# Layer one of the last two FFN blocks: seven products of half-size blocks instead of eight

## The chip, the cores and the metric

The kernel runs on one core of a Trainium2 chip. The metric is the device time of one execution in microseconds (us). PE is TensorE (matmuls), PEld its weight loads, DVE is VectorE, ACT is ScalarE, POOL is GpSimd, SP is SyncE, which issues nearly all DMAs. SBUF is the working memory, PSUM the eight accumulator banks (128 partitions x 512 fp32 each) that the matmuls write.

## The reference

```python
# attention with random features: q, k, v are (8 batches, 8 heads, 576, 64), omega is (128, 64)
q_p, k_p = phi(q_s), phi(k_s)                  # phi(x) = exp(x omega' - |x|^2/2 - max) / sqrt(128)
kv, z = einsum('bhsm,bhsd->bhmd', k_p, v), sum(k_p, axis=2)
x = num / den                                  # num = q_p kv, den = q_p z + 1e-6; x is 4608 tokens x 512
# feed-forward network (FFN)
h = x @ w_in                                   # 512 -> 2048
g = maximum(h, 0) + log1p(exp(-abs(h)))        # softplus
out = g @ w_out                                # 2048 -> 512
```

## The kernel before

**Tiling.** The 4608 tokens are cut into ten FFN blocks: two of 256 tokens, which run as a pair, and eight of 512 (`TB`). Called block 1 to block 8 here, these eight run one after the other. `w_in` and `w_out` are cut into 16 pieces of 128 hidden features (`NFC`). One step (`plan_step`) is one piece for one block: layer one makes `h` transposed, 128 hidden features x 512 tokens in one PSUM bank; ACT takes abs, exp and log, DVE adds max(h, 0) ("plus"); layer two multiplies by the piece's part of `w_out` and adds into four banks `acc`, one for each 128 tokens.

**Precision by splitting.** Each fp32 operand is held as a high and a low part (`xh`, `xl` for x; `gh`, `gl` for g; the two halves of the `wi` and `wo` tiles), and a product is three matmuls: high x high, high x low, low x high. Layer one of a step has four 128-deep chunks of x (`cc`), so 12 matmuls of 128x512 (L1040 to L1042). Layer two has four "tiles" of three matmuls each (L1069 to L1071), also 12. For each block that is 16 x 24 = 384 matmuls.

**x** lives in a ring of 1024 tokens (`RING`), that is two blocks: the attention of a later block writes x into the half of the ring that the block before last has left. x of a block comes from PE (`num` in `plan_x`, L992), which leaves it in two PSUM banks for each group of four heads; ACT rounds it to `xh` (L999) and DVE subtracts for `xl` (L1003). Attention of later batches runs between the FFN steps on all engines.

**Order.** Nothing is scheduled while the kernel runs, and each engine follows a written order. A planner (`in_order`) makes it before: every piece of work has a cost, the work that it waits for, the buffers and banks that it takes and gives back, and a due time; of what can start, the earliest due goes next. The numbers in `due + ...` and the tables `KEYS`, `QUERIES`, `IN`, `OUT` and `LATE` are its priorities. `with_fill` puts matmuls on constant data into early gaps of PE. POOL and DVE work marked `port=True` shares a port that the planner gives to one of them at a time.

**Banks.** Four of the eight banks are `acc`, two are `h` (layer one) and two are `at` (attention).

Of the kernel before, what the change touches and what calls it, by code (L numbers as in the profile page):

```python
# [10 lines left out]
F32 = mybir.dt.float32  # L11
# [8 lines left out]
P = 128  # L20
S = 576
# [11 lines left out]
AHEAD = 852.62  # L33
MARGIN = 0.00

LATE = {"num": 0.15, "turn": 52.71, "project": 0.86, "blocks": 0.82, "out": 0.35, "in": 1.69, "store": 1.22, "outer": 0.53}
# [11 lines left out]
PATIENCE = {"PE": 0.02, "DVE": 0.01, "ACT": 0.00, "POOL": 0.55, "SP": 1.42}  # L48
LEAN = {"DVE": 0.80, "POOL": 0.35, "ACT": 0.55}
KEYS = ((-43.36, -30.07, -31.94, -48.62, -93.75), (-78.36, -186.18, -77.84, -107.64, -136.45))  # L50
QUERIES = ((-77.13, -113.72, -93.37, -40.50, -2.02), (-251.59, -65.62, -225.91, -38.56, 57.66))
IN = (-72.00, -74.89, -153.56, 16.62, 44.96, -6.09, 5.92, 22.06, 77.07, 3.72, 131.98, 137.80, 388.30, 66.76, 84.33, 249.63)
OUT = (-29.34, 9.14, -28.60, 6.71, -28.19, -2.04, 43.69, 197.71, 17.60, 6.41, 70.70, 45.97, 65.95, 101.92, 218.09, 150.82)
SPREAD = ((0, 24.60), (-20.59, 57.76))
# [152 lines left out]
def favor_softplus_kernel(ctx, tc, q0, k0, qx, qy, kx, ky, vv, om, wi, wo, out):  # L207
# [104 lines left out]
    def plan_weights(nm, fc, due):  # L312
# [36 lines left out]
        def low_part(e):  # L349
# [5 lines left out]
            "SP", dma(0.65, 1.60, 1.7), due + 85.51, load, spare={} if last else {"w": 2},  # L355
# [5 lines left out]
        a = do(("ACT", "DVE"), (aw + 0.03, dw2), due + 4.63, low_bits, after=[l], port=True)  # L361
        b = do("ACT", aw + 0.03, due + 21.06, rebias, after=[l])
        c = do("DVE", dw, due + 12.79, joined, after=[a, b], port=True)
        d = do(
            ("ACT", "DVE"), (aw, dw2), due + 17.13, high_part, after=[c] + (in_w if last else []), take=[("w", box, "w")], port=True,
# [3 lines left out]
        return do(("DVE", "POOL"), (dw, pw), due + 19.28, low_part, after=[d], give=[(box, "raw")], port=True)  # L369
# [13 lines left out]
    def plan_unit(q, kind, us, due, early):  # L383
# [99 lines left out]
        def exponent(j):  # L483
# [13 lines left out]
            "SP", {"cost": 0.01, "wire": (0.0, 0.0, 2.00)} if apart else read(size), -99.0 if apart else due + 25.09, load, behind=prev.get("load"),  # L497
# [3 lines left out]
        if apart:  # L501
            ldv = [do("SP", read(P * 4 * VW), due - 47.33, lambda: nc.sync.dma_start(b["vt"], src[:, u, 1]), after=[ld])]
        if kind == "k" and not early:
            for i in range(len(us)):
                ldv.append(do(
                    "SP", dma(0.7, 1.0, 0.7), due + 76.79, lambda i=i: load_v(i), behind=ld, take=[("v", b, ("vs", i))]
                ))
        s = do(("POOL", "ACT"), (pool(w), act(w)), due + 87.38, squares, after=[ld])
        r, sm = None, [("sm", b, "sms")]
        if not cols:  # L510
            r = do("DVE", dve(w), due + 123.59, norms, after=[s], behind=prev.get("norms"), take=sm)
            prev["norms"] = r
# [31 lines left out]
        for i in range(len(us)):  # L544
            plan_queries(q, us[i], due + 27.53 * i, b, es, f"{nm}_{i}", i, i == len(us) - 1)

    def plan_split(q, kind, u, due):
# [59 lines left out]
        def exponent(t):  # L607
# [4 lines left out]
            "SP", read(n * (P + D) * P * 4), due - 147.41, load, behind=prev.get("load"), take=[("x", b, "x")],  # L612
        )
        prev["load"], ldv = ld, []
        if kind == "k":
            ldv = [do("SP", dma(0.7, 1.0, 0.7), due + 173.06, load_v, behind=ld, take=[("v", b, ("vs", 0))])]
        s = do(("POOL", "ACT"), (pool(n * D), act(n * D)), due + 105.53, squares, after=[ld])
        h = do(("ACT", "DVE"), (act(n * P), dve(n * P, 2)), due - 85.04, rounded, after=[ld], take=[("ts", b, "ts")], port=True)
        h = do(("DVE", "POOL"), (dve(n * P) + 0.12, 1.12 * pool(n * P)), due - 19.42, rest, after=[h, parted], give=[], port=True)
        r = do(  # L620
            "DVE", dve(n * D), due + 320.52, norms, after=[s, h], behind=prev.get("norms"), take=[("sm", b, "sms")],
# [4 lines left out]
            "PE", 0.118 * n, due - 37.94, project, after=[h], behind=(prev.get("project"), q.zc if kind == "q" else None),  # L626
# [5 lines left out]
        for t in range(n // 2):  # L632
            a = do(
                "ACT", act(2 * M, PSUM), due + 47.12, lambda t=t: aside(t), after=[p], behind=a,
                take=[] if t else [("ph", b, ("phs", 0))], spare={"ph": 1}, soon={} if t or n < 4 else {p: 0.22},
            )
            es.append(do("DVE", dve(2 * M), due - 26.11, lambda t=t: join(t), after=[a], give=[(b, ("ppb", t))]))
        m = do("DVE", dve(n * M), due - 38.93, maxima, after=es + [r])
        m = do("DVE", 0.33, due - 190.31, bias, after=[m], port=True)
# [20 lines left out]
    def plan_sums(q, keys, due, deps):  # L660
# [53 lines left out]
        if first:  # L714
            q.part = do("ACT", 0.29, due - 54.33, part, after=[m] + ([quads[q.n - 1].kvl] if q.n > 2 else []), give=[(y, "bank")])
            return
        a = do("DVE", 0.1, due - 223.16, z, after=[m, q.part], take=[("z", q.slots, "z")])
        q.kvl = do("DVE", 0.35, due - 64.91, whole, after=[m, a] + old, give=[(y, "bank")])
        a = do("DVE", 0.11, due + 312.18, z_turn, after=[a])
        r = do("SP", dma(2.0, 0.4, 1.4, 4), due + 87.99, out_z, after=[a], give=[(q.slots, "z")])  # L720
        q.zc = do("SP", dma(1.7, 1.6, 0.95), due - 9.18, in_z, after=[r], take=[("zb", q.slots, "zb")])

    def plan_early_keys(q, u, due, b, es):

        def outer():
# [12 lines left out]
            "PE", 0.87, due + 59.48, outer, after=es + [q.kvm], heat=2048,  # L738
# [14 lines left out]
        a = do("DVE", 0.07, due - 170.14, z, after=[q.kvm], take=[("zb", q.slots, "zb")])  # L753
        q.kvl = do("ACT", 0.32, due - 114.90, high, after=[q.kvm, a], give=[(q.slots, "kv")])
# [10 lines left out]
    def plan_queries(q, u, due, bu, es, nm, first, last):  # L765
# [46 lines left out]
        def in_blocks(qt, o, sizes):  # L812
# [13 lines left out]
            "DVE", 0.87, due + 26.67, den, after=es + [q.zc], steps=4, soon={es[1]: 0.62} if q.b > 1 and u < 4 else {},  # L826
# [475 lines left out]
```

## Time and profile before

| | us |
|---|---|
| median of 3 runs (lowest, highest) | 1007.83 (1006.66, 1009.06) |
| the profiled execution, its own time | 1009.49 |
| its span, first to last instruction | 1007.5 |
| PE busy in the span | 1000.7 (99%) |
| DVE busy, ACT busy, POOL busy | 736.3, 722.5, 173.7 |
| granted TensorE clock over the span | 1.000 of full speed (2.4 GHz) |

PE's busy time counts a matmul from its start to its modelled end. Matmuls overlap, so what a matmul costs in a row of them is read from the distance between two starts, not from its duration. Idle time of DVE or ACT costs nothing unless PE waits for it.

### The profile page before, as it was taken

Reading aid. Unit: us, or ns where it says so; the run is one execution under the profiler, and the core shown is the slowest. Engines: PE = TensorE matmul, PEld = TensorE weight load, DVE = VectorE, ACT = ScalarE, POOL = GpSimd, SP = SyncE. Lnnn points to the kernel's source line nnn. Section 1 sums busy time; section 2 is a strip of 40 time slices with the busy share of each in tenths; the row PEclk is TensorE's granted clock in tenths of the full one; section 3 lists DMA queues with packets and bytes.
Section 4 is the critical chain, followed back from the end, with each engine's and each line's share of the span. In section 5 each row is a group of like instructions: output and inputs, shape, how many; then the busy total and the mean of one; then the engine's idle time right before and its main releaser. Section 6 shows DMA issues by size and latency. Waiting matters only on the chain.

```text
span 1007.5 us, 17373 instructions
## 1 busy us (share of the span) xinstructions
PE 1000.7 (99%) x5536; PEld 842.5 (84%) x5536; DVE 736.3 (73%) x2203; ACT 722.5 (72%) x1767; POOL 173.7 (17%) x209
## 2 busy tenths in 40 slices
PE   9999999999999999999999999999999999999998
PEld 8999888888878888888878888888888888888886
DVE  5899986889889988897878778777788873223222
ACT  6999877878778878787777767777677664444443
POOL 3321332222202222422311001110002110000000
PEclk9999999999999999999999999999999999999999
DMA  9883366454465564453444433435353351001001
GB/s 344 295 286 121 105 158 157 132 149 139 119 183 153 133 171 123 151 144 108 139 127 125 125 103 110 126 93 134 95 155 92 93 123 48 1 1 42 1 1 43
DMA packets 117628, 124.50 MB, mean 124 GB/s; under 512 B 16288, under 2 KB 93728, under 8 KB 117536
## 3 DMA queue, kind: packets, MB, share of 16 engines
q1 hardware_dynamic: 117392, 123.26, 42.1%
q8 instruction: 44, 0.72, 0.3%
q14 instruction: 48, 0.39, 0.1%
q10 hardware_dynamic: 144, 0.13, 0.0%
HBM read 97.37 MB, written 25.98 MB: 122 GB/s over the span
## 4 chain that ended last, share of the span: by engine, by line
PE 96%; DMA 2%; DVE 1%; SPq 0%; ACT 0%; issue 0%; ACTq 0%
PE banks L1040 13%; PE banks L1069 13%; PE banks L1041 13%; PE banks L1042 13%; PE banks L1070 13%; PE banks L1071 13%; PE banks L673 6%; PE banks L585 5%; PE banks L992 2%; PE banks L442 1%; PE banks L732 1%; PE banks L949 1%; PE banks L872 1%; DMA rawo<-wo 1%; DMA xq<-q 1%; DMA xk<-k 0%
## 5 line engine op out<-in xcount | busy, mean ns | idle before, releaser
L1040 PE MATMUL banks<-xh,wi 128*128 128x512 f32 (+1 forms) x640 | 238.4, 372 | 0.3 <-DVE xl L926 0.3
L1041 PE MATMUL banks<-xl,wi 128*128 128x512 f32 (+1 forms) x640 | 236.2, 369 | 0.2 <-DVE xl L1003 0.2
L1042 PE MATMUL banks<-xh,wi 128*128 128x512 f32 (+1 forms) x640 | 235.9, 369 | 0.0
L1069 PE MATMUL banks<-wo,gh 128*128 128x512 f32 x576 | 228.7, 397 | 0.0
L1070 PE MATMUL banks<-wo,gh 128*128 128x512 f32 x576 | 225.1, 391 | 0.0
L1071 PE MATMUL banks<-wo,gl 128*128 128x512 f32 x576 | 224.8, 390 | 0.0
L1059 ACT CAST gh<-u 128x512 fp32r<-128x512 f32 (+1 forms) x142 | 82.7, 583 | 110.8 <-PE banks L1070 109.3
L1055 DVE SCALAR_TENSOR_TENSOR u<-banks,u 128x512 f32<-128x512 f32 (+1 forms) x160 | 101.0, 632 | 78.7 <-ACT u L1052 77.4
L1063 DVE TENSOR_TENSOR gl<-u,gh 128x512 fp32r<-128x512 f32 (+1 forms) x128 | 85.2, 666 | 88.6 <-ACT gh L1059 86.2
L1040 PEld LDWEIGHTS banks<-xh,wi 128*128 128x128 f32 x640 | 120.5, 188 | 22.2 <-issue 1.5
L1042 PEld LDWEIGHTS banks<-xh,wi 128*128 128x128 f32 x640 | 120.5, 188 | 20.7
L1041 PEld LDWEIGHTS banks<-xl,wi 128*128 128x128 f32 x640 | 120.7, 189 | 18.8 <-DVE xl L1003 0.5
L1069 PEld LDWEIGHTS banks<-wo,gh 128*128 128x128 f32 x576 | 108.2, 188 | 23.7 <-issue 4.3
L1071 PEld LDWEIGHTS banks<-wo,gl 128*128 128x128 f32 x576 | 108.1, 188 | 23.5
L1046 ACT ACTIVATE u<-banks 128x512 f32<-128x512 f32 (+1 forms) x160 | 90.0, 562 | 52.3 <-DVE gl L1063 32.2
L1070 PEld LDWEIGHTS banks<-wo,gh 128*128 128x128 f32 x576 | 108.4, 188 | 19.1
L1049 ACT ACTIVATE u<-u 128x512 f32<-128x512 f32 (+1 forms) x160 | 95.2, 595 | 3.0
L1052 ACT ACTIVATE u<-u 128x512 f32<-128x512 f32 (+1 forms) x160 | 95.0, 594 | 2.8
L609 ACT ACTIVATE phq<-phq,smq 128x128 f32<-128x128 f32 x216 | 70.4, 392 | 19.1 <-DVE smq L605 18.9
L609 ACT ACTIVATE phk<-phk,smk 128x128 f32<-128x128 f32 x216 | 71.2, 393 | 16.7 <-DVE smk L605 16.3
L781 DVE CUSTOM_DVE_ANT_0 restq<-phq,zb 128x128 f32<-128x128 f32 x280 | 72.1, 291 | 6.4 <-ACT phq L609 4.9
L791 POOL TENSOR_TENSOR phq<-phq,dnq 128x512 f32<-128x512 f32 (+1 forms) x42 | 37.8, 900 | 195.2 <-DVE dnq L787 77.9
(147 smaller groups left out, 1455.8 us busy)
## 6 DMA issues: line engine op xcount, KB each, us to landing
xk<-ky SPq DMA_DIRECT2D x48, 384.0 KB
xq<-qy SPq DMA_DIRECT2D x48, 384.0 KB
qdq<-restq SPq DMA_DIRECT2D x56, 256.0 KB
out<-o SPq DMA_DIRECT2D x36, 256.0 KB
vk<-vv SPq DMA_DIRECT2D x70, 130.0 KB
rawi<-wi SPq DMA_DIRECT2D x16, 512.0 KB
rawo<-wo SPq DMA_DIRECT2D x16, 512.0 KB
q<-qdq SPq DMA_DIRECT2D x64, 128.0 KB
```

What stands on the lines that cost most here:

```text
L609: nc.scalar.activation(b["ph"][:, c], b["ph"][:, c], AF.Exp, bias=b["sm"][:, 2, c : c + 1])
L1040: nc.tensor.matmul(b["h"], wh, xh[:, cc, t], start=cc == 0, stop=False)
L1041: nc.tensor.matmul(b["h"], wh, xl[:, cc, t], start=False, stop=False)
L1042: nc.tensor.matmul(b["h"], wl, xh[:, cc, t], start=False, stop=cc == NCC - 1)
L1046: nc.scalar.activation(b["u"], b["h"], AF.Abs)
L1049: nc.scalar.activation(b["u"], b["u"], AF.Exp, scale=-1.0)
L1052: nc.scalar.activation(b["u"], b["u"], AF.Ln, bias=1.0)
L1055: nc.vector.scalar_tensor_tensor(b["u"], b["h"], 0.0, b["u"], ALU.max, ALU.add)
L1063: return (nc.vector if e == "DVE" else nc.gpsimd).tensor_tensor(b["gl"], b["u"], b["gh"].bitcast(F32), ALU.subtract)
L1069: nc.tensor.matmul(acc[tt], gh, w2[fc][:, 0], start=fc == 0, stop=False)
L1070: nc.tensor.matmul(acc[tt], gh, w2[fc][:, 1], start=False, stop=False)
L1071: nc.tensor.matmul(acc[tt], gl, w2[fc][:, 0], start=False, stop=fc == NFC - 1)
```

## The change

The last two blocks (7 and 8) no longer run one after the other. `plan_pair` takes both at once in eight rounds (j = 0 to 7); a round treats the pieces j and j + 8 together. Layer one is then a product of two 2 x 2 block matrices: of the weights, A11 and A12 (piece j, first and second 256 rows of x's features) and A21, A22 (piece j + 8); of x, B11, B21 (block 7, first and second 256 features) and B12, B22 (block 8). In place of eight half-depth products it uses seven (Strassen's scheme in Winograd's form), six matmuls each (L1196): p1 = A11 B11, p2 = A12 B21, p3 = S4 B22, p4 = A22 T4, p5 = S1 T1, p6 = S2 T2, p7 = S3 T3.

- The weights' sums S1 to S4 are made in each round by DVE or POOL from the re-joined pieces (L1309 to L1323), and split again into high and low (L1326 to L1338); they overwrite pieces of `wi` that are no longer read, and a tile `L`.
- x's sums T1 to T4 are made once (`plan_late_x`): DVE adds and subtracts in the two PSUM banks in which block 8's x stands (L1084); ACT rounds (L1120, L1145) and DVE subtracts (L1125, L1148) for high and low parts.
- p1, p6, p5 and p3 follow each other in one bank, A, and p7 and p4 in another, C; p2 has B. Between, the bank is copied to SBUF (`copied`: s1 after p1, s2 after p6, s7 after p7; L1202) and DVE adds (`added`, L1205: c11 = B + s1, c22 = A + s7, c21 = C + s2).
- The four results go through softplus as before (`plan_g`). Block 7's g ("near") is used by layer two in the same round; block 8's g ("far") is stored over used pieces of `wi` and multiplied after the rounds, one 128-token tile after the other.
- The banks `at` are free for layer one then (`room["hp"]`), and small SBUF tiles of the attention serve as buffers (`room["two"]`).
- The planner's other priorities are new numbers throughout; of these the diff below shows two lines.

```diff
-PATIENCE = {"PE": 0.02, "DVE": 0.01, "ACT": 0.00, "POOL": 0.55, "SP": 1.42}
+PATIENCE = {"PE": 0.03, "DVE": 0.01, "ACT": 0.00, "POOL": 1.54, "SP": 1.49}
...
-            if w > 256:
+            if q.b * S + o == B * S - TB:
+                plan_late_x(q, due, o, w, any_, qc)
+            elif w > 256:
                 plan_x(q, due, o, w, any_, qc, len(kinds))
...
+        steps = {
+            3: [lambda p: tt(y[p], late["x"][:, p], ALU.subtract, p)],
+            2: [lambda p: tt(y[p], x11[0][:, p], ALU.add, p), lambda p: tt(y[p], x11[1][:, p], ALU.add, p)],
+            4: [lambda p: tt(x21[0][:, p], y[p], ALU.subtract, p), lambda p: tt(y[p], x21[1][:, p], ALU.add, p)],
+            1: [lambda p: tt(late["x"][:, p], x11[0][:, p], ALU.subtract, p), lambda p: tt(y[p], x11[1][:, p], ALU.subtract, p)],
+        }
...
+        def product(k, j, b, key, fresh):
+            if fresh:
+                b[key] = bank(f"h_{i}_{j}_{key}", b["bank", key])
+            for kk in range(2):
+                ah, al = left(k, j, b, kk)
+                bh, bl = right[k](kk)
+                for n, (x, y) in enumerate(((ah, bh), (ah, bl), (al, bh))):
+                    nc.tensor.matmul(
+                        b[key], x, y, start=fresh and not kk and not n, stop=kk == 1 and n == 2, skip_group_check=True
+                    )
+
+        def copied(e, b, key, name, nm):
+            b[name] = two(f"{name}{nm}", b["tag", name])
+            (nc.scalar.copy if e == "ACT" else nc.vector.tensor_copy)(b[name], b[key])
+
+        def added(out_, a_, b_):
+            nc.vector.tensor_tensor(out_, a_, b_, ALU.add)
...
+            p6 = prod(6, "A", False, due + 12.49, [s1, l12] + late["done"][2])
+            s2 = do(*cp, due - 35.25, lambda e, b=b, nm=nm: copied(e, b, "A", "s2", nm), after=[p6], take=[("two", b, ("tag", "s2"))])
+            p7 = prod(7, "C", True, due + 61.20, [l34] + late["done"][3], kind=hp, give=tg)
+            s7 = do(*cp, due + 21.51, lambda e, b=b, nm=nm: copied(e, b, "C", "s7", nm), after=[p7], take=[("two", b, ("tag", "s7"))])
+            p5 = prod(5, "A", False, due + 9.80, [s2] + late["done"][1], give=[(b, ("tag", "L"))])
+            c22 = do("DVE", dve(TB), due + 59.59, lambda b=b: added(b["s7"], b["A"], b["s7"]), after=[p5, s7])
+            p4 = prod(4, "C", False, due - 43.85, [s7] + late["done"][4])
+            c21 = do("DVE", dve(TB), due + 4.91, lambda b=b: added(b["C"], b["C"], b["s2"]), after=[p4, s2], give=[(b, ("tag", "s2"))])
+            p3 = prod(3, "A", False, due + 23.71, [c22] + late["B22"])
...
+        if i >= len(sizes) - 2:
+            if i == len(sizes) - 1:
+                k0_ = k
+                plan_pair(i - 1, t0 - TB, lambda j: FIRST + 2.00 * (k0_ + j * 16 / 3), chain)
+            t0 += n
+            continue
...
+    room["hp"] = room["h"] + room["at"]
+    room["th"], room["two"] = room["ph"][:4], room["ph"][4:] + room["zb"] + room["ts"] + room["t2"]
```

The first place is PE in the last two blocks. Before, a step there is layer two of one piece, of which the end stands here, and layer one of another (`wi_170` is piece 2), of which the first three matmuls stand here:

```order
L1069 MATMUL banks<-wo_1431,gh_13_10289 128x512
L1070 MATMUL banks<-wo_1431,gh_13_10289 128x512
L1071 MATMUL banks<-wo_1431,gl_13_10291 128x512
L1040 MATMUL banks<-xh,wi_170 128x512
L1041 MATMUL banks<-xl,wi_170 128x512
L1042 MATMUL banks<-xh,wi_170 128x512
```

After, this is the shortest hand-off in rounds 1 and 2: the end of p7 of round 1 (`th` is T3, `wi_448` piece 1), all of p1 of round 2 (`wi_170`), and the start of p4 of round 1 (`wi_792`, piece 9):

```order
L1196 MATMUL banks<-th_9786,wi_448 128x512
L1196 MATMUL banks<-xh,wi_170 128x512
L1196 MATMUL banks<-xl,wi_170 128x512
L1196 MATMUL banks<-xh,wi_170 128x512 x2
L1196 MATMUL banks<-xl,wi_170 128x512
L1196 MATMUL banks<-xh,wi_170 128x512
L1196 MATMUL banks<-xh,wi_792 128x512
L1196 MATMUL banks<-xl,wi_792 128x512
```

p4 goes into the bank in which p7 stands, so the copy s7 must lie between them; six matmuls of p1 stand there. Before, no matmul of a step waits for a copy of its own bank.

The second place is DVE after PE's last `num`, which brings block 8's x. Before, that is two subtractions for `xl` among the steps' plus and `gl`:

```order
L1055 SCALAR_TENSOR_TENSOR u_2_9842<-banks,u_2_9842 128x512
L1103 COPY o_0_9858<-banks 128x256
L1003 TENSOR_TENSOR xl<-banks,xh 128x512 x2
L1103 COPY o_1_9875<-banks 128x256
L1103 COPY o_2_9877<-banks 128x256
L1059 CAST gh_1_9887<-u_1_9799 128x512
L1063 TENSOR_TENSOR gl_1_9889<-u_1_9799,gh_1_9887 128x512
```

After, x's sums stand there (`b` is B22, `th` T3, `xh` and `xl` the ring, `x` block 8's first half set aside):

```order
L1148 TENSOR_TENSOR b_9740<-banks,b_9739 128x512
L1424 SCALAR_TENSOR_TENSOR u_14_9711<-banks,u_14_9711 128x512
L1084 TENSOR_TENSOR banks<-banks,x_9562 128x512
L1148 TENSOR_TENSOR b_9740<-banks,b_9739 128x512
L1084 TENSOR_TENSOR banks<-banks,x_9562 128x512
L1125 TENSOR_TENSOR th_9772<-banks,th_9771 128x512
L1084 TENSOR_TENSOR banks<-banks,xh 128x512
L1125 TENSOR_TENSOR th_9787<-banks,th_9786 128x512
L1084 TENSOR_TENSOR banks<-banks,xl 128x512
L1084 TENSOR_TENSOR banks<-banks,xh 128x512
L1428 CAST gh_14_9809<-u_14_9711 128x512
L1084 TENSOR_TENSOR banks<-banks,xl 128x512
```

The two subtractions of before have become a run of sums in the banks, and p6 of round 0 waits for the one that ends in T2.

## Rows read from the trace of the kernel before

**Rows 1.** The page's first part: busy us, share of the span, instructions.
```profile
PE 1000.7 (99%) x5536; PEld 842.5 (84%) x5536; DVE 736.3 (73%) x2203; ACT 722.5 (72%) x1767; POOL 173.7 (17%) x209
```

**Rows 2.** Stages: length, busy us of PE, PEld, DVE, ACT, POOL; PE's clock.
```profile
0.00:837.40 837.40, 835.01 (x4808) 705.73 (x4808) 688.49 (x2129) 646.21 (x1639) 173.68 (x209) 1.00 0.50 145
837.40:1003.10 165.70, 165.70 (x730) 136.73 (x729) 47.42 (x74) 75.72 (x127) 0.00 (x0) 1.00 0.04 14
...
300.00:350.00 50.00, 50.00 (x251) 41.43 (x250) 47.24 (x151) 42.06 (x112) 11.81 (x12) 1.00 0.54 147
750.00:800.00 50.00, 50.00 (x252) 42.43 (x251) 38.73 (x120) 35.68 (x83) 7.33 (x10) 1.00 0.32 87
```

**Rows 3.** All waits of PE: engine, line, releaser; us, times, longest.
```profile
PE banks L1191 <- DVE small L260: 1.1, 1, 1.1
PE banks L442 <- ACT xk L492: 0.3, 1, 0.3
PE banks L1040 <- DVE xl L926: 0.3, 1, 0.3
PE banks L992 <- DVE phk L594: 0.3, 1, 0.3
PE banks L1041 <- DVE xl L1003: 0.2, 1, 0.2
```

**Rows 4.** Timeline of the last block: start us, us, instruction; nine matmuls apart.
```profile
986.63 0.39 PE L1040 MATMUL banks<-xh,wi 128*128 128x512 f32 x1
...
988.67 0.39 PE L1040 MATMUL banks<-xh,wi 128*128 128x512 f32 x1
```

**Rows 5.** Groups by line and form, 850 to 1008: busy us, mean ns.
```profile
L1042 PE MATMUL banks<-xh,wi 128*128 128x512 f32 x104 | 40.5, 389 | 0.0
...
L1063 DVE TENSOR_TENSOR gl<-u,gh 128x512 fp32r<-128x512 f32 x29 | 20.1, 692 | 56.6 <-ACT gh L1059 56.5
...
L1055 DVE SCALAR_TENSOR_TENSOR u<-banks,u 128x512 f32<-128x512 f32 x27 | 18.7, 691 | 50.9 <-ACT u L1052 50.9
L1059 ACT CAST gh<-u 128x512 fp32r<-128x512 f32 x28 | 17.5, 624 | 57.8 <-PE banks L1070 57.8
L1049 ACT ACTIVATE u<-u 128x512 f32<-128x512 f32 x27 | 17.1, 632 | 0.8
...
L1046 ACT ACTIVATE u<-banks 128x512 f32<-128x512 f32 x27 | 16.2, 598 | 20.5 <-DVE gl L1063 20.5
...
L1059 DVE CAST gh<-u 128x512 fp32r<-128x512 f32 x1 | 0.4, 428 | 1.4 <-PE banks L1070 1.4
```

**Rows 6.** Timeline of the last microseconds: the last matmul and two copies behind it.
```profile
1002.72 0.39 PE L1071 MATMUL banks<-wo,gl 128*128 128x512 f32 x1
...
1003.15 0.42 DVE L1103 COPY o<-banks 128x256 f32<-128x256 f32 x1 [0.26 <-PE banks L1071]
1003.66 0.37 ACT L1106 COPY o<-banks 128x256 f32<-128x256 f32 x1 [0.36 <-DVE o L1103]
```

**Rows 7.** The chain that ended last, 57 to 62: start us, us, what.
```profile
59.44 1.30 DVE xl L926 x2
60.74 0.04 issue
60.78 0.39 PE banks L1040
```

**Rows 8.** Instructions of L992, PE: ns min/median/max, first and last start us.
```profile
L992 PE MATMUL banks<-q,kvs x192: 272/379/483, 142.4 to 837.1; 128*64 128x256 f32 x96, 128*64 128x192 f32 x32, 128*64 128x128 f32 x32, 128*64 128x320 f32 x32
```

**Rows 9.** Groups by form: DVE from 100 to 800, POOL over the whole span.
```profile
L1063 DVE TENSOR_TENSOR gl<-u,gh 128x512 fp32r<-128x512 f32 x75 | 53.2, 709 | 26.2 <-ACT gh L1059 24.2 <-PE banks L585 0.9
...
L791 POOL TENSOR_TENSOR phq<-phq,dnq 128x512 f32<-128x512 f32 x28 | 29.1, 1042 | 123.6 <-DVE gl L1063 28.2 <-ACT xk L565 22.4 <-ACT u L1049 20.4
L1063 POOL TENSOR_TENSOR gl<-u,gh 128x512 fp32r<-128x512 f32 x17 | 22.1, 1297 | 24.3 <-DVE dnq L781 7.2 <-ACT gh L1059 5.6 <-PE banks L585 4.6
...
L567 POOL TENSOR_TENSOR xq<-xq 128x256 f32<-128x256 f32 x20 | 12.6, 628 | 93.6 <-DVE tk L579 34.2 <-DMA qdq<-restq 19.9 <-DVE phq L791 9.9
```

More of the change, by code (lines that the diff above doesn't have):

```diff
@@ L368, in plan_weights @@
             in_w.append(d)
-        return do(("DVE", "POOL"), (dw, pw), due + 19.28, low_part, after=[d], give=[(box, "raw")], port=True)
+        return do(("DVE", "POOL"), (dw, pw), due + 18.49, low_part, after=[d], give=[(box, "raw")], port=True)
     class Quad:
@@ L611, in plan_split @@
         ld = do(
-            "SP", read(n * (P + D) * P * 4), due - 147.41, load, behind=prev.get("load"), take=[("x", b, "x")],
+            "SP", read(n * (P + D) * P * 4), due - 152.50, load, behind=prev.get("load"), take=[("x", b, "x")],
         )
@@ L615, in plan_split @@
         if kind == "k":
[L616 to L619, printed above, removed]
+            ldv = [do("SP", dma(0.7, 1.0, 0.7), due + 211.07, load_v, behind=ld, take=[("v", b, ("vs", 0))])]
+        s = do(("POOL", "ACT"), (pool(n * D), act(n * D)), due + 66.28, squares, after=[ld])
+        h = do(("ACT", "DVE"), (act(n * P), dve(n * P, 2)), due - 154.74, rounded, after=[ld], take=[("ts", b, "ts")], port=True)
+        h = do(("DVE", "POOL"), (dve(n * P) + 0.12, 1.12 * pool(n * P)), due + 0.33, rest, after=[h, parted], give=[], port=True)
         r = do(
-            "DVE", dve(n * D), due + 320.52, norms, after=[s, h], behind=prev.get("norms"), take=[("sm", b, "sms")],
+            "DVE", dve(n * D), due + 323.70, norms, after=[s, h], behind=prev.get("norms"), take=[("sm", b, "sms")],
             give=[(b, "x")],
@@ L751, in high @@
             nc.scalar.activation(q.kvs[:, :, 0:D], q.kv[:, :, 0:D], AF.Copy, scale=rm)
[L753 to L754 removed]
+        a = do("DVE", 0.07, due - 157.56, z, after=[q.kvm], take=[("zb", q.slots, "zb")])
+        q.kvl = do("ACT", 0.32, due - 138.62, high, after=[q.kvm, a], give=[(q.slots, "kv")])
     def chunks(b):
@@ L928, in plan_early_x @@
         t = do(
-            "PE", 0.45 if tail else 0.46, due - 161.70, turn, after=[d for _, d in rows], heat=1024, behind=prev.get("turn_x"),
+            "PE", 0.45 if tail else 0.46, due - 194.03, turn, after=[d for _, d in rows], heat=1024, behind=prev.get("turn_x"),
             take=[("any", y, "b")], give=[(b, "x") for b, _ in rows],
@@ L932, in plan_early_x @@
         prev["turn_x"] = t
-        h = do(("DVE", "ACT"), (dve(2 * w), act(2 * w, PSUM)), due - 167.20, high, after=[t])
-        l = do("DVE", dve(2 * w), due - 105.45, low, after=[h], give=[(y, "b")])
+        h = do(("DVE", "ACT"), (dve(2 * w), act(2 * w, PSUM)), due - 170.43, high, after=[t])
+        l = do("DVE", dve(2 * w), due - 52.32, low, after=[h], give=[(y, "b")])
         for p in range(2):
@@ L1109, in store @@
                 nc.sync.dma_start(out[t0 + tt * P : t0 + (tt + 1) * P, :], o["t"])
-            a = do("DVE", 0.34, due - 26.74, left, after=[ends[tt]], take=[("ph" if last else "t2", o, "s")])
-            r = do("ACT", 0.27, due - 108.35, right, after=[ends[tt]] if last and tt == n // P - 1 else [a], give=[(box, ("acc", i, tt))])
-            do("SP", dma(0.25, 0.8, 1.05), due - 111.08, store, after=[a, r], give=[(o, "s")], late=LATE["store"])
+            a = do("DVE", 0.34, due - 71.60, left, after=[ends[tt]], take=[("ph" if last else "t2", o, "s")])
+            r = do("ACT", 0.27, due - 107.26, right, after=[ends[tt]] if last and tt == n // P - 1 else [a], give=[(box, ("acc", i, tt))])
+            do("SP", dma(0.25, 0.8, 1.05), due - 112.46, store, after=[a, r], give=[(o, "s")], late=LATE["store"])
     assert NQ == 2
@@ L1150, in favor_softplus_kernel @@
     PAIR = 2
-    GAP = 15.46
-    PACE = 5.66
+    GAP = 7.56
+    PACE = 5.05
     t0, k, j = 0, 0, 0
```

415 lines of the change are left out of this document (350 added, 65 removed).

## The prediction

> **What bounds the kernel now.** I read the page's first part, then the busy time by stage, PE's waits, the timeline of the last block, and the groups by line. PE is busy for 1000.7 of 1007.5 us [rows 1] and in every stage shown it is busy all the time at full clock, 1.00 of 2.4 GHz [rows 2]. All its waits come to 2.0 us, of which the last, 0.2 us, is for an `xl` [rows 3]. Busy time alone would not prove a bound, since matmuls overlap; the timeline does: from 986.63 to 988.67 us nine matmuls start in 2.04 us, 0.2267 us each, while one lasts 389 ns [rows 4, 5]. From the last `num` (837.4) to the end of PE 730 matmuls take 165.7 us, 0.2270 each [rows 2]: that stage is a stream of matmuls with nothing between them. So fewer matmuls there are less time, as long as the others can still follow each other without a gap. DVE is busy for 688.5 of 837.4 us (82%) before 837.4 and 47.4 of 165.7 (29%) after it; ACT 77% and 46%; POOL does nothing after it [rows 2].
>
> **What goes.** Before, blocks 7 and 8 have 16 steps each with 12 matmuls in layer one: 384. After, 8 rounds of 7 products with 6 matmuls: 336. The written order has 4840 matmuls before and 4792 after, 48 fewer, all of 128x512, and the same 12 on constant data. 48 x 0.2267 = 10.88 us. The Trainium skill (TensorE: Matmul & The Clock Gate, Back-to-back issue gap) gives 512 columns 512/2.4 + 2.5 = 215.8 ns from start to start. Its sum would be 10.4 us, and the row, 0.2267, decides against it.
>
> **What comes on the other engines, in the rounds.** PE's work in a round is 42 matmuls of layer one and 24 of block 7's layer two, 66 x 0.2267 = 15.0 us. By the order, ACT has in the eight rounds 24 copies and 32 abs from banks or copies (598 ns), 64 exp and log (632 ns) and 34 roundings (624 ns) [rows 5]: 33.5 + 40.4 + 21.2 = 95 us of 120, 79%. DVE has 95 operations of 128x512 (692 ns), 16 of 256 columns (0.42 us, the copy in [rows 6]) and 14 quick casts (428 ns) [rows 5]: 65.7 + 6.7 + 6.0 = 78 us, 65%. Neither is the bound of a round; they hide behind PE if no single hand-off is late.
>
> **The hand-offs.** A copy must lie between two products of one bank. After the last matmul's start, 1002.72, a copy starts at 1003.15 [rows 6], 0.43 later, that is 0.20 after its slot of 0.227; the copy takes 0.60 (ACT from a bank, [rows 5]); a result reaches PE 0.04 later (60.74 to 60.78, [rows 7]). That makes 0.84 us. Of the 24 copies, eight (s7 of rounds 0, 1, 3, 4, 6, 7 and s2 of rounds 2 and 5) have six matmuls between, 1.36 us, the others twelve or more. So 0.52 us are left at the tightest, and one ACT operation (0.63) that has just started in front makes PE late by up to 0.11: eight times that is 0.9. Two in front would be 0.74, or 5.9 in all. From p4 to layer two of the same result lie at the least 24 matmuls, 5.44 us (rounds 0, 3 and 6); the chain is 0.20 + c21 0.69 + 0.60 + 0.63 + 0.63 + plus 0.69 + rounding 0.62 + low part 0.69 = 4.75, and seven hand-offs of some 0.03 to 0.09 (1003.57 to 1003.66, [rows 6]), about 5.15. That leaves 0.3. I take 0.4 us of PE waiting for all of these.
>
> **The sums of x.** They stand between the last `num` and p6 of round 0. PE has 13 tiles of layer two, p1 and p2 there, 51 matmuls, 11.56 us. DVE has 15 operations up to the last low part of T2: 14 x 0.69 + 0.43 = 10.1 us, after 0.20 for the last matmul and 0.60 for ACT's first rounding: 10.9. Two such operations in a row take 1.30 us, not 1.38 [rows 7], so 0.61 each, and then it is 9.8. The slack is 0.7 to 1.8 us. Up to p5 of round 0 DVE has 22 us and PE 25.8. One form has no row: DVE writing into a bank (14 sums, six of them ahead of p6, and 16 of the L1205 sums). The nearest rows are a bank read at 691 ns and two SBUF operands at 692; the low end is the quick cast, 428 ns, the high end two passes, 1.38 us. At the low end p6 waits for nothing. At the high end p6 is late by 6 x 0.69 less the slack, 2.3 to 3.4 us, p5 by 14 x 0.69 - 3.8 = 5.9 in all, and with c21 0.69 longer three rounds lose 0.4 each: 7.1. I take 0.69, since both rows agree on it, and 0.5 us of waiting at p6 for the chance that it is a little more.
>
> **Attention ends earlier.** Block 8's x is now needed before round 0. After the last `num` PE has 60 + 336 + 384 = 780 matmuls, 176.8 us, where it had 165.7; with an end 10 us earlier its last matmul must start at some 816 (1002.95 - 10 - 176.8) instead of 837.1 [rows 8]. DVE's 688.5 us then need 84% of the time instead of 82% [rows 2]. At 94% of DVE (300 to 350) PE still had no gap [rows 2]; I take nothing, and the price if this cover is gone is a rival below.
>
> **The rest.** The other priorities change the order only slightly ahead of the first FFN step: the same DMAs, a few swapped, and the same number of matmuls ahead of it. With waits of 2.0 us in all [rows 3] there is at most that to gain, and I take 0 with 1.5 either way. The end keeps its chain (matmul, two half copies one after the other, store); the last store is now alone, where four followed each other; I take 0 and up to 0.4 less.
>
> **The sum**, against the profiled execution: 1009.49 - 10.88 + 0.4 + 0.5 = 999.5. The median of the runs is 1.66 below that execution, so 997.8 us.
>
> **Rivals.**
> *PE waits in the rounds or at p6* for what is added above: speaking for it, the tight places and the form without a row; against it, 79% and 65%. Price 3 to 8 us (5.9 by the copies, 7.1 by the sums): 1000 to 1005.
> *POOL takes DVE's port.* POOL has 41 operations in the rounds: 22 by 1.04 to 1.30 us, 16 by 0.63 and 3 low parts by 1.30, some 40 us of 120 [rows 9]. If a DVE operation with two SBUF operands must wait for POOL's to end, it meets one in a third of the cases and waits 0.65 on average; the 16 low parts of block 7's g have the least cover: 16 x 0.33 x 0.65 = 3.4 us, so 1000.4. The rows speak against it: the same DVE operation takes 709 ns where POOL works and 692 where it does nothing [rows 5, 9], 17 ns, that is 0.9 us for some 55 such operations on an engine with 35% free. The Trainium skill (SBUF — State Buffer, Who interferes with whom) says that the two engines share a port pair and that the later one waits out the other's whole instruction when a DVE instruction has two SBUF inputs. By that rule this rival holds wherever the written order does not keep the two apart; the trace so far shows only the 17 ns.
> *Slower: attention does not get done earlier.* If DVE, at 94% in places, can't be packed closer, p6, p7 and p4 of round 0 wait for block 8's x. All 21 us unabsorbed give 997.8 + 21 = 1019; the change loses from 11 us on, half of it, and with 15 it is 1013. Against it: DVE is free for 149 us before 837.4 [rows 2].
> *It doesn't do what it says*, because PE isn't bound by matmuls: against it 0.2270 us over 730 of them. The time would be 1008.
>
> **Chances.** The forecast 0.70, with a range of its own of 995.5 to 1000 (no waits and 1.5 less from the order: 995.5; 2 us more of waits: 1000). Waits in the rounds 0.17; POOL's port 0.05; slower 0.04; no change 0.04. The range, 995.0 to 1003.0, leaves out the upper part of the second case and the two last. A measurement of this kernel can tell 0.2%, 2 us, from no change: faster 0.92, same 0.04, slower 0.04.
>
> **What would show it.** Right: the last stage of PE with starts 0.227 apart and 780 matmuls after the last `num`, whose last matmul starts at 813 to 818; PE's waits under 3 us in all; L1084 and L1205 at 0.65 to 0.75 us. The second case would show PE waiting on L1196 for ACT s (L1202) or on DVE (L1125), the third DVE low parts well over 0.7 us, the fourth one long wait at round 0. The prediction is wrong if PE waits for 5 us or more in the last two blocks, or if its stream there is not 0.227 apart.

## The result, and the profile after

The changed kernel took 994.88 us (median of four runs, 994.32 to 997.79) where the kernel before, on the same chip, took 1008.44 (1006.66 to 1014.88): ratio 0.986, interval 0.9812 to 0.9908. That is 13.6 us less where 10 were forecast, and 0.12 us under the range. The profiled execution after took 997.79 us, 11.70 less than the one before (1009.49). The first thing to settle is why these two differences aren't the same.

The first part of the page after, to set beside [rows 1]:

```profile
PE 989.3 (99%) x5488; PEld 832.2 (84%) x5488; DVE 772.7 (78%) x2273; ACT 729.7 (73%) x1801; POOL 235.2 (24%) x261
```

48 matmuls fewer; DVE and POOL do 36 and 62 us more, and PE is still busy for 99% of the span. The stages after (length, busy us of PE, PEld, DVE, ACT, POOL; PE's clock), beside [rows 2], the first from behind the last `num` to the end of PE:

```profile
813.94:992.14 178.20, 178.20 (x782) 146.37 (x780) 93.62 (x157) 99.25 (x179) 47.53 (x44) 1.00 0.05 17
850.00:900.00 50.00, 50.00 (x220) 41.03 (x219) 29.61 (x49) 33.64 (x60) 21.36 (x22) 1.00 0.00 0
```

The rounds are a stream of matmuls too, 0.2273 us each in the second row. All waits of PE, beside [rows 3]:

```profile
PE banks L1568 <- DVE small L260: 1.1, 1, 1.1
PE banks L442 <- ACT xk L492: 0.8, 1, 0.8
PE banks L1409 <- DVE xl L928: 0.3, 1, 0.3
PE banks L994 <- DVE phk L594: 0.3, 1, 0.3
PE banks L1409 <- DVE u L1424: 0.2, 1, 0.2
```

L1196 is not among them: no product waits. They come to 2.7 us in all (forecast: under 3). The `num` of block 8 (L1045, instruction by line: ns min/median/max, first and last start), beside [rows 8]:

```profile
L1045 PE MATMUL banks<-q,kvs x32: 379/379/430, 790.6 to 813.6; 128*64 128x256 f32 x32
```

The last starts at 813.6, where 816 (813 to 818) was forecast. The new forms on DVE from 800 on (busy us, mean ns), beside [rows 5, 9]:

```profile
L1205 DVE TENSOR_TENSOR banks<-banks,s 128x512 f32<-128x512 f32 x16 | 11.1, 696 | 8.6 <-PE banks L1196 8.6
...
L1084 DVE TENSOR_TENSOR banks<-banks,xl 128x512 f32<-128x512 f32 x6 | 4.2, 692 | 0.1
...
L1084 DVE TENSOR_TENSOR banks<-x,xh 128x512 f32<-128x512 f32 x2 | 2.1, 1070 | 0.0
```

DVE writing into a bank takes 0.69 us, as taken; the 1070 has another cause (below). The end, beside [rows 6]:

```profile
991.75 0.39 PE L1255 MATMUL banks<-wo,wi 128*128 128x512 f32 x1
992.18 0.37 ACT L1271 COPY o<-banks 128x256 f32<-128x256 f32 x1 [10.09 <-PE banks L1255]
992.58 0.42 DVE L1268 COPY o<-banks 128x256 f32<-128x256 f32 x1 [10.90 <-ACT o L1271]
```

The last matmul starts 10.97 us earlier than before. From it to the end of the span are 4.25 us where there were 4.77.

**The start is the surprise.** The first matmul of layer one, at 60.78 before [rows 7], starts at 59.44 after, though the written order of PE is the same up to 13 us. Busy time by stretch from 5 to 20 us, of before:

```profile
5.00:10.00 5.00, 5.00 (x42) 4.25 (x40) 2.56 (x7) 3.22 (x9) 2.80 (x4) 1.00 1.08 359
10.00:15.00 5.00, 5.00 (x35) 4.15 (x37) 2.25 (x7) 2.92 (x11) 3.94 (x8) 1.00 1.10 370
15.00:20.00 5.00, 4.88 (x70) 4.75 (x66) 3.54 (x12) 3.59 (x13) 0.12 (x1) 1.00 1.03 392
```

and of after:

```profile
5.00:10.00 5.00, 5.00 (x42) 4.25 (x40) 2.56 (x7) 3.17 (x9) 2.69 (x4) 1.00 1.08 361
10.00:15.00 5.00, 5.00 (x49) 4.15 (x51) 2.64 (x9) 2.91 (x11) 2.89 (x6) 1.00 1.08 374
```

PE is busy all the time in both, but gets through 35 matmuls from 10 to 15 us in the one and 49 in the other. The clock column says 1.00 there, yet the trace has no record of a granted clock before 17.2 us in before and 13.4 us in after; until then the matmuls are twice as far apart: the first 128x512 ones, on constant data, start 0.43 us from each other, where [rows 4] have 0.2267. PE runs at 1.2 GHz first, and the moment it goes to 2.4 GHz was another in these two executions.

### The profile page after: what moved, and what is told of

Read it like the earlier page. It is cut to its first block, busy times and chain, and to the rows that moved or that the text cites. A ratio compares the mean times of both kernels' runs of the same rounds, so it can differ in the third digit from the quotient of the medians.

```text
span 996.0 us, 17456 instructions
## 1 busy us (share of the span) xinstructions
PE 989.3 (99%) x5488; PEld 832.2 (84%) x5488; DVE 772.7 (78%) x2273; ACT 729.7 (73%) x1801; POOL 235.2 (24%) x261
## 4 chain that ended last, share of the span: by engine, by line
PE 96%; DVE 1%; ACT 1%; DMA 1%; issue 0%; SPq 0%; ACTq 0%
PE banks L1409 10%; PE banks L1438 10%; PE banks L1410 10%; PE banks L1411 10%; PE banks L1439 10%; PE banks L1440 10%; PE banks L1196 8%; PE banks L673 5%; PE banks L585 5%; PE banks L1254 3%; PE banks L1253 3%; PE banks L1255 3%; PE banks L442 2%; PE banks L994 2%; PE banks L732 1%; PE banks L951 1%
## 5 line engine op out<-in xcount | busy, mean ns | idle before, releaser
L1409 PE MATMUL banks<-xh,wi 128*128 128x512 f32 (+1 forms) x512 | 189.0, 369 | 0.5 <-DVE xl L928 0.3
L1410 PE MATMUL banks<-xl,wi 128*128 128x512 f32 (+1 forms) x512 | 186.3, 364 | 0.1
L1411 PE MATMUL banks<-xh,wi 128*128 128x512 f32 (+1 forms) x512 | 186.1, 363 | 0.0
L1438 PE MATMUL banks<-wo,gh 128*128 128x512 f32 x448 | 178.2, 398 | 0.0
L1439 PE MATMUL banks<-wo,gh 128*128 128x512 f32 x448 | 175.3, 391 | 0.0
L1440 PE MATMUL banks<-wo,gl 128*128 128x512 f32 x448 | 175.0, 391 | 0.0
L1409 PEld LDWEIGHTS banks<-xh,wi 128*128 128x128 f32 x512 | 96.4, 188 | 18.4 <-issue 2.3
L1411 PEld LDWEIGHTS banks<-xh,wi 128*128 128x128 f32 x512 | 96.4, 188 | 15.6
L1410 PEld LDWEIGHTS banks<-xl,wi 128*128 128x128 f32 x512 | 96.6, 189 | 13.6 <-DVE xl L1005 0.4
L1438 PEld LDWEIGHTS banks<-wo,gh 128*128 128x128 f32 x448 | 84.2, 188 | 18.1 <-issue 3.4
L1439 PEld LDWEIGHTS banks<-wo,gh 128*128 128x128 f32 x448 | 84.4, 188 | 14.1
L1424 DVE SCALAR_TENSOR_TENSOR u<-banks,u 128x512 f32<-128x512 f32 (+1 forms) x128 | 78.8, 617 | 18.9 <-ACT u L1421 17.9
L1432 POOL TENSOR_TENSOR gl<-u,gh 128x512 fp32r<-128x512 f32 (+1 forms) x45 | 49.8, 1109 | 112.9 <-ACT gh L1428 60.2
L1421 ACT ACTIVATE u<-u 128x512 f32<-128x512 f32 (+1 forms) x128 | 74.8, 585 | 1.4
L1418 ACT ACTIVATE u<-u 128x512 f32<-128x512 f32 (+1 forms) x128 | 74.9, 585 | 1.2
L1432 DVE TENSOR_TENSOR gl<-u,gh 128x512 fp32r<-128x512 f32 (+1 forms) x83 | 53.0, 639 | 23.2 <-ACT gh L1428 21.9
```

Source lines behind the costliest of these rows:

```text
L1409: nc.tensor.matmul(b["h"], wh, xh[:, cc, t], start=cc == 0, stop=False)
L1410: nc.tensor.matmul(b["h"], wh, xl[:, cc, t], start=False, stop=False)
L1411: nc.tensor.matmul(b["h"], wl, xh[:, cc, t], start=False, stop=cc == NCC - 1)
L1418: nc.scalar.activation(b["u"], b["u"], AF.Exp, scale=-1.0)
L1421: nc.scalar.activation(b["u"], b["u"], AF.Ln, bias=1.0)
L1424: nc.vector.scalar_tensor_tensor(b["u"], b["h"], 0.0, b["u"], ALU.max, ALU.add)
```

## The experiments

Theory S: that moment differs from execution to execution of either kernel, and the forecast's sum holds at an equal start. Theory P, the rival: the new priorities make the start 2 to 3 us shorter each time. Seven profiled executions, in columns: the time at which the trace's first record of a granted clock stands (called the record here); first layer-one matmul; from it to the last `num`; from there to the last matmul; from there to the span's end; span (us).

| execution | record | layer one | to `num` | to last | end | span |
|---|---|---|---|---|---|---|
| before | 17.2 | 60.78 | 776.3 | 165.66 | 4.77 | 1007.5 |
| before (e5) | 17.1 | 60.78 | 776.8 | 165.65 | 4.79 | 1008.0 |
| after | 13.4 | 59.44 | 754.2 | 178.12 | 4.25 | 996.0 |
| after (e1) | 5.2 | 56.15 | 754.1 | 178.12 | 4.25 | 992.6 |
| after (e14) | 31.2 | 66.04 | 754.5 | 178.12 | 4.25 | 1002.9 |
| before, 9 constant matmuls (e13) | 5.8 | 56.98 | 776.8 | 165.66 | 4.78 | 1004.2 |
| after, 9 constant matmuls (e10) | 6.3 | 57.21 | 754.2 | 178.11 | 4.25 | 993.8 |

The three rows of after alone show the start moving by 9.9 us with the record. A straight line through two of them (59.44 at 13.4 and 66.04 at 31.2) gives 60.9 for a record at 17.2, where before has 60.78, and with 9 constant matmuls the two kernels' starts lie 0.2 apart. So at an equal record neither kernel starts earlier. The record is not quite all: in e4, below, it stands at 4.3 and layer one at 56.95, some 0.9 us later than that line; PE waits 0.8 us for a DMA there.

**Both kernels again** (no edit).

> The changed kernel once more, beside the kernel before, to see whether the 13.6 us of the first comparison hold and what the profiled execution's start does. Matmuls alone: 48 x 0.2267 = 10.9 us. Theory S (the excess is in the first 25 us, where TensorE's clock came up 3.9 us earlier in the profiled execution of after than in that of before, and this differs from execution to execution of either kernel): the gain comes out anywhere from 10.5 to 13.5 us, and another profiled execution has its first clock record at another time, with the first layer-one matmul moved by up to 1.5 us along with it. Theory P (the new priorities give some 2.5 us each time): the gain is again 13 to 14 us and the first layer-one matmul again starts at 59.4 us.

Measured: 994.98 (993.82 to 1005.39), ratio 0.9889 (0.9851 to 0.9927). Its timeline has the first layer-one matmul 3.3 us earlier than the first profile of the same kernel, and from there on the two agree within 0.1 us:

```profile
56.15 0.39 PE L1409 MATMUL banks<-xh,wi 128*128 128x256 f32 x1 [0.31 <-DVE xl L928]
```

Its stretches from 5 us on:

```profile
5.00:10.00 5.00, 5.00 (x59) 3.94 (x57) 4.18 (x11) 4.08 (x13) 2.73 (x4) 1.00 1.07 362
10.00:15.00 5.00, 4.97 (x80) 4.75 (x80) 3.90 (x15) 5.00 (x21) 2.87 (x6) 1.00 1.09 371
```

80 matmuls where the other two had 49 and 35. The start moves with the execution, as S says, and by more than the 1.5 us that S had allowed; the median, though, is P's.

> The kernel before once more, one profiled execution. In the five profiles so far whose order ahead of the first layer-one matmul is that of before or after, the first layer-one matmul starts at 56.2 us where the clock's record begins at 5.2 us, at 59.4 for 13.4, 60.4 for 16.1, 60.8 for 17.2 and 67.2 for 33.7. If the start depends on that time alone and not on the kernel: it lies within 0.5 us of 56.2 + 0.4 x (time of the record - 5.2), and from the first layer-one matmul to the last matmul it is again 941.9 us, 0.2 either way. If the priorities of after make the start shorter by themselves: the first layer-one matmul is 1 to 3 us later than that line.

Measured: record at 17.1, layer one at 60.78 (the line gives 61.0), 942.4 us from there to the last matmul (forecast 941.9, 0.2 either way: 0.3 outside). Before's start lies on the line again, though at nearly the same record as in its first profile (17.2), so this is a repeat more than a new point.

> The changed kernel for the third time. Of its ten executions so far eight lay at 993.8 to 996.4, while the kernel before and the two others with after's start lie half of the time 3 us and more above their lowest. If it was luck that after's ten started early: about half of the new runs lie above 996.5 and the median comes out at 995.5 to 999. If after's start is better by itself: at most one in six above 996.5 and the median again at 994 to 995.

Measured: 997.01 (994.64 to 1003.81), ratio 0.9866 (0.9832 to 0.9901), three of six above 996.5: luck, by this. Its profiled execution shows a second effect, the granted clock falling again (busy time by stretch, clock in the third column from the end):

```profile
15.00:20.00 5.00, 4.49 (x57) 4.12 (x56) 4.14 (x16) 4.72 (x19) 0.69 (x2) 0.89 1.00 368
20.00:25.00 5.00, 5.00 (x36) 4.90 (x34) 3.33 (x12) 3.18 (x10) 1.43 (x3) 0.50 1.03 407
25.00:30.00 5.00, 5.00 (x49) 4.65 (x49) 3.68 (x10) 3.94 (x13) 0.00 (x0) 0.93 1.04 387
```

It had risen at 5.3 us, fell at 18.9 for 6.8 us, and layer one started at 59.81 instead of 56.15.

> The changed kernel once more. Its sixteen executions so far have a mean of 996.7, 2.9 us above their lowest; those of before a mean 4.9 us above their lowest, and those of the two kernels with after's start and 48 more matmuls 4.6 and 5.2. If only the lot of sixteen was good: the six new ones have a mean of 997 to 1001, with at least two above 998. If after starts better by itself: a mean of 995 to 997 again and at most one above 998.

Measured: twelve runs, median 1001.31, mean 1000.6, eight of them above 998; ratio 0.9911 (0.988 to 0.9941). So the good times of the sixteen were the luck of the lot.

**A steadied start.**

```diff
-    fill("at.0", 5, idle)
+    fill("at.0", 14, idle)
```

> After with 14 instead of 5 matmuls on constant data at the very start: 9 more at 0.427 us, 3.8 us, so PE starts real work at 6.9 to 7.3 instead of 3.5 us unless the clock rises in between. If the time at which the clock rises is fixed by what PE does then (the first operations have 128 and 56 columns and 64 rows): the record begins before 9 us in the profiled execution, and the six runs lie within 2 us of each other, at 994 to 997, with none above 999. If it is a matter of the execution alone: the runs spread by 5 to 12 us as before and lie 2 to 4 us later.

Measured: 996.02, four runs within 995.84 to 996.07 and two at 999.12 and 999.44 (mean clock 0.996); the record began at 5.7 us. By this profile and the narrow times, what PE does at the start sets when the clock rises. Two runs stand above 999 where none was expected, at the mean clock that e11's execution with the fall shows.

> The kernel before with the same 14 matmuls on constant data at the start as in the run of after with them, which had four of six times within 995.84 to 996.07. This takes the start out of the comparison. If the change's own gain is what is left at an equal start (941.9 to 942.4 less 932.3 from the first layer-one matmul to the last matmul, and 0.5 at the end): 10.4 us, so most runs within 1006.0 to 1007.0, and a few 3.4 us above. If the new priorities also bring 2 to 3 us at the start: most runs at 1008.5 to 1009.5. If the clock's rise isn't held by the longer start, the runs spread by over 8 us.

The same edit in before. Measured: 1007.55 (1006.19 to 1011.9). The eight runs without the fall have a median of 1007.2, 11.3 us above the four of after; half of them lie in S's range and none in P's. The other four, with the fall (it stands at 20.0 us in the profile), lie at 1010.3 to 1011.9.

> After with 9 matmuls on constant data at the start, half way between 5 and 14. Four more at 0.427 us are 1.7 us of which a part falls into time that PE would wait or run at half rate anyway. If the longer start alone brings the clock up early: most runs within 0.5 us of each other at 994 to 995.3, so 1 us under the run with 14, and no run above 999. If 9 are too few: a spread of 5 to 12 us as with 5.

The same line with 9. Measured: 995.35, five runs at 994.55 to 995.58, one at 997.74. Four lie within 0.4 us of each other and none above 999, as expected. Ratio to the kernel before, which keeps its 5: 0.9846 (0.9819 to 0.9873).

> The kernel before with 9 matmuls on constant data at the start, beside after with the same 9, whose six runs lay at 994.55 to 995.58 and one at 997.74 (mean clock 0.996). Change alone at an equal start: 10.7 us (first layer-one matmul to last matmul 942.1 against 932.1, end 0.5, around the span 0.2), so most runs at 1005.2 to 1006.5 and the ones with the clock's fall at 1008.4 to 1009.5. If after's new priorities give 2 to 3 us more at the start: most runs at 1007.5 to 1008.5.

The same in before. Measured: eight runs at 1005.26 to 1006.64 (median 1006.07), four with the fall at 1008.42 to 1009.12. Beside e10: 1006.07 - 995.22 = 10.85 us without the fall, and 1008.6 - 997.7 = 10.9 with it (one run of after). At an equal start the change is worth 10.8 us with 9 constant matmuls, 11.3 with 14. P, which asks for some 13, is out.

The fill planner allowed one more matmul where it sees no gap:

```diff
-EXTRA = 0.21
+EXTRA = 1.50
```

> After with 9 matmuls on constant data at the start and three more of them later: two behind the first projection (about 5 us) and one at about 17 us, where PE waits 0.5 us for ACT and in two profiled executions the granted clock fell to half 2 us later and cost 3.6 us. If the fall depends on what PE does there: none of the six runs shows a mean clock of 0.997 or less, and all lie within 1 us of each other at 995 to 996 (the three cost 0.2 to 0.9 us). If it doesn't: one or two of six again lie 2.5 to 3.6 us above the others at 0.996.

Measured: 995.89; 995.52 to 995.90 four times, 999.37 and 1000.6 at a clock of 0.996 and 0.995. The profiled execution, without the fall, has the third matmul at 19.1 us, 2.8 behind PE's wait of 0.5 us and not in it. So the fall does not go away with these matmuls, but whether that wait brings it was not tested; its cause is open.

**The priorities.** Alone, with the last two blocks one after the other:

```diff
-            if q.b * S + o == B * S - TB:
+            if False:
...
-        if i >= len(sizes) - 2:
+        if False:
```

> The new priorities alone: blocks 7 and 8 run one after the other with eight half-depth products' worth of matmuls, as before, and all numbers of the planner are those of after. Theory S: within 1 us of the kernel before (1007 to 1009). Theory P: 2 to 3 us faster than before (1005 to 1006). As these numbers were not made for two blocks one after the other, some waits of 1 to 3 us in the last stage are possible; they would show in PE's waits and are taken off.

Measured: 1009.09 (eleven runs, 1004.74 to 1016.57; a twelfth, of 2007.46, twice as long for a reason not known, is left out), ratio 1.0018 (0.9987 to 1.0049). The profiled execution had its record at 33.7 us and layer one at 67.23; from there to the last matmul 942.65 us, where before has 941.9 to 942.5. Nothing gained, though the last `num` starts 762.7 us after the first layer-one matmul, where before has 776.3: the new numbers bring the attention forward by themselves. Then the seven products with before's numbers in all shared code (two of the lines, shown against the changed kernel):

```diff
-PATIENCE = {"PE": 0.03, "DVE": 0.01, "ACT": 0.00, "POOL": 1.54, "SP": 1.49}
+PATIENCE = {"PE": 0.02, "DVE": 0.01, "ACT": 0.00, "POOL": 0.55, "SP": 1.42}
```

> Seven products with the numbers of before in all code that the two kernels share. Theory S: 10.9 us faster than before, 1 us either way (996 to 998), if PE's waits stay under 1 us. Theory P: 2 to 3 us slower than after (997 to 998) at any start. If the old numbers don't bring block 8's attention forward, the wait at p6, p7 or p4 of round 0 shows as one long wait of PE, up to 20 us, and the time is 1000 to 1017.

Measured: 1021.6, ratio 1.0135 (1.0109 to 1.0161), slower than before and above all three forecasts. The last `num` starts 781.7 us after the first layer-one matmul (after: 754.2), PE's waits begin so:

```profile
PE banks L1045 <- DMA q<-qdq: 4.3, 2, 2.6
PE banks L1196 <- DVE t1l L1125: 1.9, 1, 1.9
```

and while PE waits its clock falls to half, from 838.7 for 3.4 us and from 852.3 for 10.2 us (stretches, same columns as above):

```profile
835.00:850.00 15.00, 8.70 (x31) 4.64 (x32) 7.27 (x12) 5.45 (x10) 7.63 (x9) 0.89 0.23 46
850.00:865.00 15.00, 11.60 (x33) 7.70 (x32) 11.96 (x21) 6.44 (x12) 0.03 (x1) 0.66 0.00 0
```

The new numbers give nothing alone; without them the change loses 22 us (954.2 to 932.3, first layer-one to last matmul), because block 8's attention isn't done in time. PE's waits of L1045, L1196 and L1253 are 10.9 of these 22 us; the rest goes with the half clock, 12 more constant matmuls that the planner put in and wider starts, and was not separated.

**The rounds.** p2 computed twice:

```diff
-            for kk in range(2):
+            for kk in (0, 1) * (2 if k == 2 else 1):
```

> After with p2 computed twice into its bank in each round: eight products of six matmuls, 48 more matmuls in all, every other instruction and its place as in after. If PE's issue is the bound of the rounds: 48 x 0.2267 = 10.9 us more than after (1005 to 1006.5). If other engines' hand-offs set the pace of the rounds and the saved matmuls had only made room: less than 8 us more.

Measured: the stretch from the last `num` to the last matmul is 189.00 us against 178.12: 10.88 us for 48 matmuls, the forecast to the second digit. Its row, beside the first of the stages after:

```profile
810.83:999.92 189.09, 189.09 (x830) 155.37 (x828) 95.55 (x158) 100.21 (x179) 47.52 (x44) 1.00 0.04 16
```

So fewer matmuls in the rounds are less time, one for one. (The times, 1005.21 to 1016.68, median 1010.95, are spread by the start, so they don't decide it.) The copies s7 and s2 made twice:

```diff
-            (nc.scalar.copy if e == "ACT" else nc.vector.tensor_copy)(b[name], b[key])
+            for _ in range(1 if name == "s1" else 2):
+                (nc.scalar.copy if e == "ACT" else nc.vector.tensor_copy)(b[name], b[key])
```

> After with the copies s7 and s2 made twice each, one behind the other, all else in place: 16 more operations of 0.60 us on ACT in the rounds, 87% of it instead of 79%. If the tight hand-offs had some 0.5 us left, as worked out: the eight are late by 0.1 us or more each, so the stretch from the last num to the last matmul is 0.8 to 3 us longer than after's 178.1 (more, up to 6, if another ACT operation stands in front), and PE's waits name L1203 or the copies. If they had much more left: 178.1 within 0.2, and no such wait.

Measured: 181.43 us, 3.3 more, and PE now waits for the copies. The row of its waits, and two matmuls at one of the four places (0.82 us apart instead of 0.23):

```profile
PE banks L1196 <- ACT s L1203: 1.3, 4, 0.4
...
860.13 0.39 PE L1196 MATMUL banks<-xh,wi 128*128 128x512 f32 x1
860.95 0.50 PE L1196 MATMUL banks<-xh,wi 128*128 128x512 f32 x1 [0.43 <-ACT s L1203]
```

In the trace, matmuls start late at exactly the eight places that the prediction named. At four it is by 0.08 to 0.10 us, so of the 0.60 us that the second copy takes 0.50 were covered there: the slack of 0.52 that the prediction worked out. At the other four the copies are held up by another ACT operation in front, and the matmuls are late by 0.36 to 0.60. The start after each late one is late by another 0.11; together these are 3.2 of the 3.3 us. POOL's work of the last two blocks moved to DVE:

```diff
-        dp = lambda n: (("DVE", "POOL"), (dve(n), pool(n)))
+        dp = lambda n: (("DVE", "POOL"), (dve(n), 1000.0))
...
-            l = do(("DVE", "POOL"), (dve(n), pool(n)), due + 40.29, low, ...
+            l = do(("DVE", "POOL"), (dve(n), 1000.0), due + 40.29, low, ...
```

> After with POOL's 41 operations of the last two blocks (weights' sums, low parts) on DVE, so that POOL does nothing there. If POOL's work held up DVE's by whole operations (the rival with 3.4 us): the stretch from the last num to the last matmul gets shorter than after's 178.1, towards 177.0, and DVE's low parts of g go from over 0.70 to 0.69 us. If not: 178.1 within 0.3, with DVE busy some 28 us more in the stretch.

Measured: 179.48 us, 1.4 longer, neither case's number, though block 8's low parts of g do go from a mean of 786 to 687 ns. PE waits 0.5 and 0.2 us for DVE, which is busy 17.7 us more:

```profile
PE banks L1196 <- DVE wi L1338: 0.5, 1, 0.5
...
PE banks L1196 <- DVE u L1222: 0.2, 1, 0.2
```

Late starts around these waits make up the rest. So POOL's work does not lengthen the rounds; moved to DVE it does.

## Why the prediction was right in its sum and wrong in its time

- *48 matmuls, 10.88 us*: right, 10.88 by e4.
- *Waits of 0.4 at the hand-offs and 0.5 at p6*: PE waits for neither. The 0.9 is spent all the same: the stretch after the last `num` is 1.29 us over 780 x 0.2267 (before: 0.39 over 729), as some 170 of the starts are 230 to 240 ns apart instead of 227 (before: some 35). Why these are, no run shows. The size came out right by luck, its reason was wrong.
- *DVE into a bank, 0.69*: right for 13 of 14 sums of x.
- *Attention ends at 813 to 818*: right, 813.6 (815.0 if layer one had started where before's did). DVE is busy for 678.7 us up to the end of the last `num`, 83% of the time, where 84% was worked out; so it could be packed closer. The rival's price (21 us, up to 1019) is near the 22 that e3 paid.
- *Other priorities 0, 1.5 either way*: right alone (e2), but they are what makes the line above true (e3).
- *The end, 0 to 0.4 less*: 0.53 less.
- The sum was -10.0 us. At an equal start the traces show -9.9 from the first layer-one matmul to the last (932.3, mean of four executions, against 942.2 of four), -0.5 behind it and -0.2 around the span: -10.6; the runs with the steadied start show -10.8 and -11.3. So the sum itself was 0.6 to 1.3 short, 0.5 of it the end.
- **The step that failed** is the last: "The median of the runs is 1.66 below that execution, so 997.8 us". It took PE's start as the same in every execution, and gave it no term in the range. That start moves layer one between 55.9 and 67.2 us, and with it the whole time. In before's profiled execution the clock rose at 17 us, in after's at 13, and after's other three runs, 2.4 to 3.5 us below that one, must have started earlier still, if the distances of the table hold for them; they have no profile. Over all comparisons after has 28 runs from 993.82 to 1006.02, median 996.8, mean 998.4, before 90 runs from 1004.75 to 1016.3, median 1009.5, mean 1009.7. Of all ways to take four of the 28 runs, one in eight has a median under 995.0, and 95 in 100 have one between 994.4 and 1004.3. So 994.88 was a lucky lot, and the forecast of 997.8 lies between the median and the mean of all 28; that it lies so near is luck too, as two errors offset each other: the sum was short, and the median of three runs of before that it was taken from lay 2 us under before's mean. The rows of before had it to see: 42 and 35 matmuls in 5 us of a fully busy PE, then 70, and runs 2.4 us apart.
- *POOL takes DVE's port* (chance 0.05): the mechanism is real, the price of 3.4 us wasn't paid. The prediction read a mean of 709 against 692 ns [rows 9] as 17 ns for each; in the trace of before four of those 75 took 1.04 to 1.10 us and the others 0.65 to 0.72. One of the four, and POOL's operation that it met (two timelines):

```profile
360.11 1.07 DVE L1063 TENSOR_TENSOR gl<-u,gh 128x512 fp32r<-128x512 f32 x1
...
360.02 0.62 POOL L567 TENSOR_TENSOR xk<-xk 128x256 f32<-128x256 f32 x1 [1.79 <-issue]
```

After, DVE's timeline:

```profile
831.37 1.46 DVE L1084 TENSOR_TENSOR banks<-x,xh 128x512 f32<-128x512 f32 x1
```

and POOL's:

```profile
830.98 1.29 POOL L1234 TENSOR_TENSOR gl<-u,gh 128x512 fp32r<-128x512 f32 x1 [3.04 <-ACT gh L1229]
```

DVE's sum, both operands in SBUF, ends 0.56 us after POOL's operation; with POOL's work gone (e7) both such sums take 0.69. The Trainium skill (SBUF — State Buffer, Who interferes with whom) says that of a DVE instruction with two SBUF inputs and a GpSimd instruction that reads SBUF the later one waits out the other's whole instruction. The trace agrees: after the last `num` seven such DVE operations of 128x512 met one of POOL, and all ended 0.55 to 0.56 us after it, while the 31 two-operand ones with a bank among their operands that met one took 0.68 to 0.70 us as always. Of the seven three were held by 0.8 us each and two by 0.09, with DVE far from late.

## What to carry to other kernels

When PE starts are evenly spaced, count matmuls: 48 of them came out at 10.88 us, to the hundredth. The hand-offs of a seven-product scheme made PE wait for nothing while six matmuls (1.36 us) covered one copy of 0.60 us; with two copies there (e6) they did. Where the start of an execution varies, compare two kernels from a common event behind the start to the last instruction as well as by their medians; here that distance repeats within 0.7 us while the times spread by 12. And look behind a mean that is a little high: a few held operations tell more than an even 2%.

## What was not expected of the hardware

- With PE busy from 1 us on, its clock rose from 1.2 to 2.4 GHz between 4.2 and 33.7 us in sixteen profiled executions. Nine instead of five 128x512 matmuls ahead of the small ones brought it to 4.2 to 6.3 us in each of three profiles, 14 to 5.7 and 6.4 in two; in the eleven with five it lies anywhere from 4.3 to 33.7. After's 28 runs with five spread over 12.2 us, its six with nine over 3.2 (e10, median 995.35, the lowest of the versions with a longer start) and six more over 5.1 (e12).
- The printed clock is 1.00 where the trace has no record yet; the number of matmuls in a stretch shows the true one.
- The clock can fall again shortly after the rise: in two profiles (e11, e9) at 18.9 and 20.0 us, with PE 90% busy in the 5 us before, for 6.8 us, at a cost of 3.6 us. Three more constant matmuls up to that point (e12) did not prevent it.
